# Retention and two feed-forward layers on one core: weight steps freed from program order, the first weight loads moved, the tail of v in tiles of its own

## The chip, the cores and the metric

One core of a Trainium2 chip. The metric is the device time of one execution in microseconds; the median of several executions counts. The profile is of one execution, and its span runs from the first to the last instruction.

## The reference

A retention block feeds two feed-forward layers. For batch 4, 8 heads, 576 positions and head size 64, `scores = q k^T / 8` is multiplied by a lower-triangular table of powers of a decay (one for each head), and the product is multiplied by `v`. The heads are laid side by side, which makes `x` of 2304 tokens by 512. Then:

```python
h = x @ w_in                                   # 512 x 2048
g = (a0 + a1*h + a2*h**2 + a3*h**3) / (1 + abs(b0)*abs(h) + abs(b1)*h**2 + 1e-6)
x = g @ w_out                                  # 2048 x 512
h = x @ w2_in
g = s * maximum(h, 0)**2 + b
out = g @ w2_out
```

q, k, v and the result are float32; the four weight matrices come as float64 and are cut by the kernel into two parts (wh and wl) whose sum carries the precision, as the activations are.

## The kernel before, in words

**Retention.** Work goes by pairs of heads: 16 pairs (4 batches by 4 pairs), and two neighbouring pairs form a group that is loaded together, 8 groups in all. `loads(g)` (L320) takes the tiles of group g from pools of three buffers and issues 15 DMAs on SyncE's queue: for k, q and v four loads of 128 positions by 4 heads (L196), and one load for the last 64 positions, the tail (L203). The tails of k and q lie in one tile (`raw_t`, 64 rows each). The tail of v is loaded as the last 128 positions (S - 128 to S) into a fifth chunk of v's tile; its first 64 rows are positions that the fourth chunk holds already, and the mask makes them count for nothing. `scale(p)` (L212) multiplies the v of a pair by its decay on GpSimd, all five chunks in one instruction. The loop over pairs (L357) then does, for pair p, in this order: load group p/2 + 2 (for even p), the state's part of the values (`value_state`, L294), the transpositions of pair p + 2 (tails first, L229, then k and q, L224) with its scaling, the sums of pair p + 1 (`state`, L268, with copies on ScalarE, L282, and sums on VectorE, L284), the values (`value_chunk`, L306, and the scaled outputs on VectorE, L308 and L309), the scores of pair p + 1 (L247, L249) and their masks on VectorE (L253, L256). PE's and VectorE's instructions of this part are pinned.

**Pins.** The kernel is written in a framework that puts the instructions of each engine in order at build, by a simulated timeline: an instruction that is ready there may be put before others that stand ahead of it in the program. `keep_in_program_order` pins an instruction behind the one that was written just before it on its engine. A pinned instruction cannot come before that one; if that one is not pinned itself, both may be put forward together.

**Weights.** One weight tile is 128 columns of w_in with the 128 rows of w_out that belong to them, 1 MB of float64; there are 16 for each layer, 32 in all. `w_load(kf)` (L96) issues two DMAs of 512 KB on SyncE (L100, L102) into one of two raw buffers. `w_cut(kf)` (L104) turns the raw tile into wh and wl in five steps, a generator that stops after each: ScalarE's Abs (L116) and VectorE's clamp of the low words (L117); VectorE's L119 and L120; L122; L125; then ScalarE's copy to wh (L132), GpSimd's difference wl (L133), and the load of the next tile, which takes the raw buffer that is now free. One buffer `wm` holds the intermediate value.

The first three tiles are cut within the retention, one call of the generator at the end of each pair from pair 2 on, all steps pinned. The last stop of one tile runs on into the first step of the next, so a tile takes four calls and three tiles take 13. The loads of the first two tiles stand in pair 0 behind `loads(2)`, the third group (L360). Four small loads (`small_loads`, L314) of parameters stand in pair 2; from them come `babs` (L599, ScalarE) and `aneg` (L600, VectorE), which are written after the retention and not pinned. Tiles 3 to 31 are cut within the feed-forward, where `emit_cuts` (L549) spreads the steps over the units of work; there L116, L117 and L119 are pinned, the others are not.

**Feed-forward.** A unit is one block of 512 (or 256) tokens with one weight tile: 12 matmuls in (L412 to L414), the function on ScalarE, VectorE and GpSimd (L429 to L463, or L465 to L473), 12 matmuls out (L497). In the function of the first layer, L453 is VectorE's last read of the PSUM tile that a later unit's L412 needs.

Of the kernel before, what the change touches and what calls it, by code (L numbers as in the profile page):

```python
# [10 lines left out]
F32 = mybir.dt.float32  # L11
# [5 lines left out]
ALU = mybir.AluOpType  # L17
# [13 lines left out]
RAW_BUFS = 2  # L31
# [4 lines left out]
W_FIRST = 3  # L36
# [4 lines left out]
def retention_ffn_kernel(ctx, tc, q, k, v, w_in1, w_out1, a, b, w_in2, w_out2, s2, b2, maskv, gdec, out):  # L41
    nc = tc.nc
    B, H, S, D = q.shape
    NT, DM = out.shape
    DFF = w_in1.shape[1]
    P = 128
# [3 lines left out]
    NCH = (S + P - 1) // P  # L50
    TAIL = S - (NCH - 1) * P
    NMAIN = S // P
# [23 lines left out]
    def f32(t):  # L76
        return t.bitcast(F32)
# [8 lines left out]
    def next_load():  # L86
        if w_ahead:
            w_load(w_ahead.pop(0))
# [15 lines left out]
    def w_cut(kf, pinned=False):  # L104

        words = w_raw.pop(kf).rearrange("p w n -> p (w n)").bitcast(I32).rearrange("p (n two) -> p n two", two=2)
        lo, hi = words[:, :, 0].bitcast(U32), words[:, :, 1]
        f = hi.bitcast(F32)  # L110
        m = wtmp.tile([P, 2 * DM], F32, tag="wm", name=f"wm{kf}")
        t = m.bitcast(I32)

        pin = tc.keep_in_program_order
        rest = pin if pinned else lambda ins: ins
        pin(nc.scalar.activation(m, f, AF.Abs))  # L116
        pin(nc.vector.tensor_scalar(lo, lo, 2.0 ** 28, 2.0 ** 32 - 256, op0=ALU.add, op1=ALU.min))  # L117
        yield
        pin(nc.vector.tensor_scalar(m, m, 2.0 ** -15, None, op0=ALU.max))  # L119
        rest(nc.vector.tensor_scalar(t, t, 5, 2, op0=ALU.logical_shift_left, op1=ALU.logical_shift_right))  # L120
        yield
        rest(nc.vector.scalar_tensor_tensor(out=t, in0=hi, scalar=-0x40000000, in1=t,  # L122
                                            op0=ALU.bitwise_and, op1=ALU.bitwise_or))
        yield
        rest(nc.vector.scalar_tensor_tensor(out=hi.bitcast(U32), in0=lo, scalar=29, in1=t.bitcast(U32),  # L125
                                            op0=ALU.logical_shift_right, op1=ALU.bitwise_or))
        yield
        wh, wl = w_slots[kf % W_BUFS]
        whf, wlf = (x.rearrange("p w c f -> p (w c f)") for x in (wh, wl))
        for which in range(2):  # L130
            w_t[kf, which] = (wh[:, which], wl[:, which])
        nc.scalar.copy(whf, f)  # L132
        nc.gpsimd.tensor_tensor(out=wlf, in0=f, in1=f32(whf), op=ALU.subtract)  # L133
        next_load()
# [8 lines left out]
    def retention(actx):  # L143

        sb1 = actx.enter_context(tc.tile_pool(name="sb1", bufs=1))
# [7 lines left out]
        NM = NMAIN * P  # L153
        mv = sb1.tile([P, P + TAIL + NCH * H + NP], F32, name="mv")
        mask, tmask = mv[:, 0:P], mv[:, P:P + TAIL]
        vdec = mv[:, P + TAIL:P + TAIL + NCH * H].rearrange("p (c h) -> p c h", c=NCH)
# [8 lines left out]

        assert 2 * TAIL == P and NCH == NMAIN + 1 and NP % 2 == 0
        tiles, xT, pm, pv = {}, {}, {}, {}

        def raw(nm, p):

            h = 2 * (p % 2)
            return tiles[nm, p // 2][:, :, h:h + 2, :]

        def flat(t):
            return t.rearrange("p h d -> p (h d)")


        def pe(ins):
            tc.keep_in_program_order(ins)
# [1 line left out]
        dve = pe  # L181

        def load_tiles(g):
            for nm, n in (("k", NMAIN), ("q", NMAIN), ("v", NCH), ("t", 1)):
                tiles[nm, g] = sbr.tile([P, n, 4, D], F32, tag=f"raw_{nm}", name=f"raw_{nm}{g}")

        def load(nm, g, part, eng=nc.sync):

            bb, h0 = pairs[2 * g][0], 2 * pairs[2 * g][1]
            src = {"q": q, "k": k, "v": v}[nm]  # L190
            t = tiles[nm, g]
            hs = range(4) if part is None else range(2 * part, 2 * part + 2)
            h1, h2 = hs[0], hs[-1] + 1
            if part is None:
                for c in range(NMAIN):
                    eng.dma_start(out=t[:, c], in_=src[bb, h0:h0 + 4, c * P:(c + 1) * P, :].rearrange("h p d -> p h d"))  # L196
            else:
                for j in hs:
                    eng.dma_start(out=t[:, 0:NMAIN, j, :],
                                      in_=src[bb, h0 + j, 0:NM, :].rearrange("(c p) d -> p c d", p=P))  # L200
            s0 = S - P if nm == "v" else NM
            o = t[:, NMAIN] if nm == "v" else tiles["t", g][0:TAIL, 0] if nm == "k" else tiles["t", g][TAIL:P, 0]
            eng.dma_start(out=o[:, h1:h2, :], in_=src[bb, h0 + h1:h0 + h2, s0:S, :].rearrange("h p d -> p h d"))  # L203

        def decay_table():

# [4 lines left out]

        def scale(p):  # L212
            hp = pairs[p][1]
            t = raw("v", p)
            nc.gpsimd.tensor_tensor(out=t, in0=t, op=ALU.mult,
                                    in1=vdec[:, :, 2 * hp:2 * hp + 2].unsqueeze(3).to_broadcast([P, NCH, 2, D]))

        def transpose(p):
            o = xT[p]
# [76 lines left out]

        def value_chunk(p):
            bb, hp = pairs[p]
            vn = raw("v", p)
            for c in range(NCH):  # L300
                n = min(P, S - c * P)
                for j in range(2):
                    r = slice(64 * j, 64 * j + 64)
                    o = pv[p][r, c * P:c * P + n] if c < NMAIN else out_tail[r]
                    rh = pm[p, j][:, c * P:c * P + n] if c < NMAIN else pm[p, 2][:, j, :]
                    pe(nc.tensor.matmul(o, lhsT=vn[:, c, j, :], rhs=rh, start=False, stop=True, skip_group_check=True))  # L306
            x = sbt.tile([P, S], F32, tag="x", bufs=2, name=f"x{p}")
            dve(nc.vector.tensor_tensor(out=x[:, NM:S], in0=out_tail, in1=odec[:, hp, NM:S], op=ALU.mult))  # L308
            dve(nc.vector.tensor_tensor(out=x[:, 0:NM], in0=pv[p], in1=odec[:, hp, 0:NM], op=ALU.mult))  # L309
            xs = slice(bb * S, (bb + 1) * S)  # L310
            nc.scalar.copy(xh[:, hp, xs], x)
            nc.gpsimd.tensor_tensor(out=xl[:, hp, xs], in0=x, in1=f32(xh[:, hp, xs]), op=ALU.subtract)
# [44 lines left out]
        for p in range(NPAIR):  # L357
            if p % 2 == 0:
                loads(p // 2 + 2)
            if p == 0:  # L360
                for _ in range(RAW_BUFS):
                    next_load()
            if p == 2:
                small_loads()
            value_state(p, range(1, NMAIN))
            if 0 < p < NPAIR - 2:
                transposes(p + 2)
            value_state(p, [NMAIN])
            if p + 1 < NPAIR:
                state(p + 1)  # L370
            value_chunk(p)
            if p + 1 < NPAIR:
                scores(p + 1)
            if p == 0:
                transposes(2)
            if p > 1:
                next(steps, None)
        for _ in steps:
            pass
# [217 lines left out]
    with ExitStack() as actx:  # L597
        retention(actx)
# [49 lines left out]
```

## Time and profile before

| | us |
|---|---|
| median of 3 runs | 941.04 (940.54 to 942.96) |
| the profiled execution | 942.34 |
| its span | 940.1 |
| PE busy in the span | 896.5 (95%) |
| VectorE, ScalarE, GpSimd busy | 619.3, 556.4, 357.7 |
| mean granted clock of PE | 0.983 |

In the profile PE is the matmuls, PEld the weight loads into PE, DVE is VectorE, ACT is ScalarE, POOL is GpSimd and SP is SyncE, whose whole work here is to issue DMAs (SPq). L12 is line 12. A row of the timeline gives the start, the duration, the engine, the line and the operation with the names of what it writes and reads; in brackets stands how long the engine was idle before it and what ended that. Rows of the same kind that follow each other are merged (x4). [...]

### The profile page before, as it was taken

To read this page: it belongs to the slowest core of one execution; us is meant where nothing else is said; L and a number is where in the kernel's file an instruction comes from. 1 tells how busy PE (TensorE), PEld (TensorE's weight loads), DVE (VectorE), ACT (ScalarE), POOL (GpSimd) and SP (SyncE) were. 2 spreads that over 40 slices of the span, in tenths; PEclk is the share of its full clock that TensorE was granted. 3 is DMA by queue.
4 is the path that set the end of the run, shared out by engine and by line. 5 is a ranking of instruction groups with operands and counts; after the bars stand their busy time and mean duration, and the time that the engine had idled before them with its cause. 6 is when DMAs were issued, how large, how long until landed. Compare 5 with 4: busy or idle time off the path is not lost.

```text
span 940.1 us, 12896 instructions
## 1 busy us (share of the span) xinstructions
PE 896.5 (95%) x4912; PEld 756.0 (80%) x4912; DVE 619.3 (66%) x965; ACT 556.4 (59%) x940; POOL 357.7 (38%) x256
## 2 busy tenths in 40 slices
PE   7799899999999989999799999999999999999998
PEld 6688778888787868888588878888888888888886
DVE  2476679688796796988688984446555555554344
ACT  3354389796777677777768864544444443443332
POOL 4355457456474454665557871111111111110000
PEclk9899899999999989999999999999999999999999
DMA  8978112011110111100111111111111102100013
GB/s 190 230 165 199 43 46 83 7 46 45 36 35 20 46 45 46 45 26 21 46 45 45 46 45 46 45 45 46 45 45 45 45 2 89 45 0 1 1 68 134
DMA packets 84716, 54.16 MB, mean 58 GB/s; under 512 B 61232, under 2 KB 78256, under 8 KB 84656
## 3 DMA queue, kind: packets, MB, share of 16 engines
q1 hardware_dynamic: 82784, 52.68, 19.0%
q10 hardware_dynamic: 1872, 0.68, 0.3%
q8 instruction: 38, 0.62, 0.3%
q14 instruction: 22, 0.18, 0.1%
HBM read 48.62 MB, written 4.72 MB: 57 GB/s over the span
## 4 chain that ended last, share of the span: by engine, by line
PE 74%; DVE 9%; ACT 5%; POOL 4%; issue 3%; SPq 2%; DMA 2%; DVEq 0%; POOLq 0%; ACTq 0%
PE o L497 34%; PE h L412 12%; PE h L413 12%; PE h L414 12%; POOL tq L434 2%; DVE acc L509 2%; SPq L196 2%; PE pv L306 1%; DVE tt L451 1%; PE b_sum L268 1%; DVE h L452 1%; PE sc L247 1%; PE pv L294 1%; DVE wm L122 1%; POOL wl L133 1%
## 5 line engine op out<-in xcount | busy, mean ns | idle before, releaser
L412 PE MATMUL h<-xl,wh 128*128 128x512 f32 (+1 forms) x640 | 236.8, 372 | 9.8 <-DVE tt L453 9.7
L413 PE MATMUL h<-xh,wl 128*128 128x512 f32 (+1 forms) x640 | 237.2, 371 | 1.4 <-POOL wl L133 1.4
L414 PE MATMUL h<-xh,wh 128*128 128x512 f32 (+1 forms) x640 | 237.0, 370 | 0.0
L133 POOL TENSOR_TENSOR wl<-raw,wh 128x1024 fp32r<-128x1024 f32 x32 | 78.3, 2446 | 292.5 <-ACT wh L132 151.7
L412 PEld LDWEIGHTS h<-xl,wh 128*128 128x128 f32 x640 | 121.4, 190 | 32.5 <-DVE tt L453 4.0
L434 POOL TENSOR_TENSOR tq<-tq,ta 128x512 f32<-128x512 f32 (+1 forms) x80 | 100.8, 1262 | 111.4 <-ACT tq L433 104.4
L413 PEld LDWEIGHTS h<-xh,wl 128*128 128x128 f32 x640 | 121.5, 190 | 23.6 <-POOL wl L133 2.8
L468 ACT ACTIVATE ta<-h 128x512 f32<-128x512 f32 (+1 forms) x80 | 44.2, 555 | 161.0 <-PE h L414 160.3
L414 PEld LDWEIGHTS h<-xh,wh 128*128 128x128 f32 x640 | 121.5, 190 | 20.6
L470 DVE TENSOR_SCALAR tt<-ta,s_sb,b_sb 128x512 f32<-128x512 f32 (+1 forms) x80 | 45.1, 566 | 137.6 <-ACT ta L469 137.4
L497 PE MATMUL o<-gl,wh 128*128 128x512 f32 (+1 forms) x320 | 119.5, 374 | 6.5 <-POOL gl L463 5.0
L463 POOL TENSOR_TENSOR gl<-tt,gh 128x512 fp32r<-128x512 f32 (+1 forms) x80 | 105.5, 1321 | 46.1 <-ACT gh L458 37.3
L497 PE MATMUL o<-gh,wl 128*128 128x512 f32 (+1 forms) x320 | 118.4, 370 | 0.0
L497 PE MATMUL o<-gh,wh 128*128 128x512 f32 (+1 forms) x320 | 117.9, 369 | 0.0
L497 PE MATMUL o<-wh,gl 128*128 128x512 f32 x288 | 112.1, 389 | 0.0
L497 PE MATMUL o<-wh,gh 128*128 128x512 f32 x288 | 112.1, 389 | 0.0
L473 DVE TENSOR_TENSOR gl<-tt,gh 128x512 fp32r<-128x512 f32 (+1 forms) x80 | 69.5, 870 | 42.6 <-ACT gh L472 42.6
L497 PE MATMUL o<-wl,gh 128*128 128x512 f32 x288 | 93.1, 390 | 1.4 <-DVE acc L509 1.4
L509 DVE TENSOR_TENSOR acc<-acc,o 128x512 f32<-128x512 f32 (+1 forms) x114 | 70.1, 650 | 12.0 <-PE o L497 12.0
L440 DVE TENSOR_TENSOR tt<-tt,h 128x512 f32<-128x512 f32 (+1 forms) x80 | 50.1, 627 | 41.4 <-ACT tt L435 41.3
L497 PEld LDWEIGHTS o<-gl,wh 128*128 128x128 f32 x320 | 60.6, 189 | 19.5 <-POOL gl L463 6.6
L451 DVE SCALAR_TENSOR_TENSOR tt<-tt,aneg,h 128x512 f32<-128x512 f32 (+1 forms) x80 | 55.0, 687 | 28.4 <-ACT h L446 28.4
(74 smaller groups left out, 1514.1 us busy)
## 6 DMA issues: line engine op xcount, KB each, us to landing
raw<-in_moe_w_in_dram SPq DMA_DIRECT2D x32, 512.0 KB, 3.9
raw<-in_moe_w_out_dram SPq DMA_DIRECT2D x32, 512.0 KB, 4.8
raw_v<-in_v_dram SPq DMA_DIRECT2D x39, 128.0 KB, 3.0
out_dram<-acc SPq DMA_DIRECT2D x18, 256.0 KB, 2.1
raw_k<-in_k_dram SPq DMA_DIRECT2D x32, 128.0 KB, 3.2
raw_q<-in_q_dram SPq DMA_DIRECT2D x30, 128.0 KB, 3.0
raw_t<-in_k_dram SPq DMA_DIRECT2D x7, 64.0 KB, 3.3
raw_t<-in_q_dram SPq DMA_DIRECT2D x7, 64.0 KB, 3.4
```

What stands on the lines that cost most here:

```text
L133: nc.gpsimd.tensor_tensor(out=wlf, in0=f, in1=f32(whf), op=ALU.subtract)
L412: nc.tensor.matmul(ps, lhsT=wh[:, c, :], rhs=xl[:, c, r], start=c == 0, stop=False)
L413: nc.tensor.matmul(ps, lhsT=wl[:, c, :], rhs=xh[:, c, r], start=False, stop=False)
L414: nc.tensor.matmul(ps, lhsT=wh[:, c, :], rhs=xh[:, c, r], start=False, stop=c == NC - 1)
L434: nc.gpsimd.tensor_tensor(out=tq, in0=tq, in1=ta, op=ALU.mult)
L440: nc.vector.tensor_tensor(out=tt, in0=tt, in1=h, op=ALU.mult)
L451: nc.vector.scalar_tensor_tensor(out=tt, in0=tt, scalar=aneg[:, 0:1], in1=r, op0=ALU.add, op1=ALU.mult)
L463: nc.gpsimd.tensor_tensor(out=gl, in0=tt, in1=f32(gh), op=ALU.subtract)
L470: nc.vector.tensor_scalar(tt, ta, s2_sb, b2_sb, op0=ALU.mult, op1=ALU.add)
L473: nc.vector.tensor_tensor(out=gl, in0=tt, in1=f32(gh), op=ALU.subtract)
L497: nc.tensor.matmul(ps, lhsT=lh, rhs=rh, start=st and x == 0, stop=sp and x == 2)
L509: nc.vector.tensor_tensor(out=at, in0=at, in1=ps, op=ALU.add)
```

## The change

Three edits. (1) In `w_cut` the pins of L116, L117 and L119 hold only for tiles 0 to 4 (`W_FIRST + RAW_BUFS` is 5); the steps of tiles 5 to 31 are not pinned at all. (2) In the retention's loop the first two weight loads go from pair 0 to pairs 3 and 5, the small loads from pair 2 to pair 7, and the steps of the first three tiles begin at pair 5 (one call a pair up to pair 11, two from pair 12 on: 15 calls). (3) The tail of v is loaded as its 64 positions alone, into rows 64 to 127 of three standing tiles that are cleared once at the start; the scaling becomes two instructions, one for four chunks and one for the tail.

```diff
@@ w_cut
-        pin = tc.keep_in_program_order
-        rest = pin if pinned else lambda ins: ins
+        def free(ins):
+            return ins
+
+        rest = tc.keep_in_program_order if pinned else free
+        pin = tc.keep_in_program_order if kf < W_FIRST + RAW_BUFS else free
@@ retention
+        vtail = [sb1.tile([P, 4, D], F32, name=f"vtail{i}") for i in range(3)]
+        for t in vtail:
+            nc.gpsimd.memset(t[0:P - TAIL], 0.0)
+        def tail_of(p):
+            h = 2 * (p % 2)
+            return vtail[p // 2 % 3][:, h:h + 2, :]
@@ load_tiles
-            for nm, n in (("k", NMAIN), ("q", NMAIN), ("v", NCH), ("t", 1)):
+            for nm, n in (("k", NMAIN), ("q", NMAIN), ("v", NMAIN), ("t", 1)):
@@ load
-            s0 = S - P if nm == "v" else NM
-            o = t[:, NMAIN] if nm == "v" else tiles["t", g][0:TAIL, 0] if nm == "k" else tiles["t", g][TAIL:P, 0]
-            eng.dma_start(out=o[:, h1:h2, :], in_=src[bb, h0 + h1:h0 + h2, s0:S, :].rearrange("h p d -> p h d"))
+            o = vtail[g % 3][P - TAIL:] if nm == "v" else tiles["t", g][0:TAIL, 0] if nm == "k" else tiles["t", g][TAIL:P, 0]
+            eng.dma_start(out=o[:, h1:h2, :], in_=src[bb, h0 + h1:h0 + h2, NM:S, :].rearrange("h p d -> p h d"))
@@ scale
-            t = raw("v", p)
+            t, vt = raw("v", p), tail_of(p)[P - TAIL:]
             nc.gpsimd.tensor_tensor(out=t, in0=t, op=ALU.mult,
-                                    in1=vdec[:, :, 2 * hp:2 * hp + 2].unsqueeze(3).to_broadcast([P, NCH, 2, D]))
+                                    in1=vdec[:, 0:NMAIN, 2 * hp:2 * hp + 2].unsqueeze(3).to_broadcast([P, NMAIN, 2, D]))
+            nc.gpsimd.tensor_tensor(out=vt, in0=vt, op=ALU.mult, in1=vdec[P - TAIL:, NMAIN, 2 * hp:2 * hp + 2]
+                                    .unsqueeze(2).to_broadcast([TAIL, 2, D]))
@@ value_chunk
-            vn = raw("v", p)
+            vn, vt = raw("v", p), tail_of(p)
-                    pe(nc.tensor.matmul(o, lhsT=vn[:, c, j, :], rhs=rh, start=False, stop=True, skip_group_check=True))
+                    pe(nc.tensor.matmul(o, lhsT=vn[:, c, j, :] if c < NMAIN else vt[:, j, :], rhs=rh,
+                                        start=False, stop=True, skip_group_check=True))
@@ the loop over pairs
-            if p == 0:
-                for _ in range(RAW_BUFS):
-                    next_load()
-            if p == 2:
+            if p in (3, 5):
+                next_load()
+            if p == 7:
                 small_loads()
@@
-            if p > 1:
+            for _ in range((p > 4) + (p > 11)):
                 next(steps, None)
```

## Rows read from the trace of the kernel before

**Rows 1.** Stretches: us; PE, PEld, DVE, ACT, POOL busy (instructions); PEclk; DMA share; GB/s:
```profile
0.00:116.82 116.82, 96.78 (x1168) 88.72 (x1168) 65.52 (x145) 49.64 (x104) 54.06 (x46) 0.93 0.72 166
116.82:560.00 443.18, 424.10 (x2013) 353.43 (x2012) 364.18 (x551) 344.01 (x571) 271.88 (x198) 0.98 0.12 41
```

**Rows 2.** Timeline of PE in the retention: L229 opens a pair's transpositions:
```profile
33.88 0.27 PE L229 MATMUL trt<-ident,raw_t 128*128 128x128 f32 x1
...
44.18 0.45 PE L229 MATMUL trt<-ident,raw_t 128*128 128x128 f32 x1 [2.88 <-DMA raw_t<-in_q_dram]
...
51.62 0.27 PE L229 MATMUL trt<-ident,raw_t 128*128 128x128 f32 x1
...
56.85 0.29 PE L229 MATMUL trt<-ident,raw_t 128*128 128x128 f32 x1
...
79.39 0.27 PE L229 MATMUL trt<-ident,raw_t 128*128 128x128 f32 x1
...
93.27 0.27 PE L229 MATMUL trt<-ident,raw_t 128*128 128x128 f32 x1
...
98.83 0.69 PE L294 MATMUL b_out<-xT,spad 128*128 128x64 f32 x2 [4.28 <-DVE pmt L253]
...
105.14 0.27 PE L229 MATMUL trt<-ident,raw_t 128*128 128x128 f32 x1
```

**Rows 3.** Timeline of SyncE's queue, 0 to 112 us:
```profile
20.24 2.16 SPq L196 DMA_DIRECT2D raw_k<-in_k_dram  x4
...
28.89 0.52 SPq L100 DMA_DIRECT2D raw<-in_moe_w_in_dram  x1
...
31.29 5.66 SPq L196 DMA_DIRECT2D raw_k<-in_k_dram  x4
...
44.85 0.50 SPq L315 DMA_DIRECT2D a_sb<-in_moe_a_dram  x1
...
92.52 0.37 SPq L100 DMA_DIRECT2D raw<-in_moe_w_in_dram  x1
```

**Rows 4.** Busy time by stretch, 31.2 to 36 us (columns as in rows 1):
```profile
31.20:36.00 4.80, 4.80 (x69) 4.39 (x67) 2.95 (x8) 1.28 (x4) 3.87 (x3) 1.00 0.98 348
```

**Rows 5.** Timelines of ScalarE, VectorE and GpSimd in the retention:
```profile
36.45 1.20 ACT L116 ACTIVATE wm<-raw 128x1024 f32<-128x1024 f32 x1 [1.94 <-DMA raw<-in_moe_w_out_dram]
...
47.74 0.76 DVE L600 TENSOR_SCALAR aneg<-a_sb 128x4 f32<-128x4 f32 x1 [3.75 <-DMA a_sb<-in_moe_a_dram]
...
97.95 0.70 DVE L117 TENSOR_SCALAR raw<-raw 128x1024 uint32<-128x1024 uint32 x1 [5.50 <-DMA raw<-in_moe_w_out_dram]
...
87.19 2.94 POOL L215 TENSOR_TENSOR raw_v<-raw_v,mv 128x640 f32<-128x640 f32 x2 [6.41 <-PE trt L229]
```

**Rows 6.** Line L203, the tails' loads: issue ns min/median/max; time to landing:
```profile
L203 SPq DMA_DIRECT2D raw_t<-in_k_dram x9: 607/607/2019, 1.8 to 74.5; - x9
L203 SPq DMA_DIRECT2D raw_v<-in_v_dram x9: 368/505/1612, 4.9 to 88.9; - x9
...
DMA to landing us min/median/max: 2.3/3.2/6.8
```

**Rows 7.** First layer: waits in total, VectorE's and PE's timeline, sum at half clock:
```profile
PE h L412 <- DVE tt L453: 9.7, 5, 3.7
...
323.11 0.68 DVE L119 TENSOR_SCALAR wm<-wm 128x1024 f32<-128x1024 f32 x1
...
325.57 1.66 DVE L122 SCALAR_TENSOR_TENSOR wm<-raw,wm 128x1024 int32<-128x1024 int32 x1
...
333.21 0.77 PE L412 MATMUL h<-xl,wh 128*128 128x512 f32 x1 [3.65 <-DVE tt L453]
...
sum 13.65, PE 12.55 PEld 9.19 DVE 13.65 ACT 8.38 POOL 10.36; mean PE 4.18 PEld 3.06 DVE 4.55 ACT 2.79 POOL 3.45
```

**Rows 8.** Timeline of GpSimd at the start of the retention:
```profile
8.21 1.04 POOL L209 TENSOR_TENSOR odec<-odec,mv 128x512 f32<-128x512 f32 x1 [6.02 <-DMA raw_v<-in_v_dram]
9.21 1.26 POOL L215 TENSOR_TENSOR raw_v<-raw_v,mv 128x640 f32<-128x640 f32 x1
```

## The prediction, made before the change was run

> **What bounds the kernel now.** I read the busy time by stretch first [rows 1]. The program has three stretches: the retention (0 to 116.82 us), the first feed-forward layer (to about 560 us) and the second. In the third PE is busy throughout, so nothing in this change can move it. In the first layer PE is busy 424.10 of 443.18 us: 19.1 us idle. In the retention PE is busy 96.78 of 116.82 us and the granted clock is 0.93 in the mean.
>
> Then I followed one mark of the retention, the transposition of the tails (L229), which opens the PE work of each pair of heads [rows 2]. From 51.62 to 56.85 a pair takes 5.23 us with no wait; I take that as the unhindered pair. Against it three places lose time. A: from 33.88 to 51.62 two pairs take 17.74 us, 7.28 too many, with a wait of 2.88 us for the tail of q and a granted clock of one half behind it. B: from 51.62 to 79.39 five pairs take 27.77 us (1.62 too many) and from 79.39 to 93.27 two take 13.88 (3.42 too many), 5.04 together; it falls at the two changes of weight tile. C: from 93.27 to 105.14 one pair takes 11.87 us, 6.64 too many, with a wait of 4.28 us for VectorE's L253.
>
> The queue of SyncE says why A happens [rows 3]. Loads are issued there one behind the other without a pause from the start to about 89 us. The first two weight tiles are issued at 28.89, between the third group of heads and the fourth; the four loads of k that follow take 5.66 us to issue where the group before took 2.16, since the transfers are full (348 GB/s, share 0.98 [rows 4]). ScalarE too waits 1.94 us there for the first weight tile before its first step on it [rows 5].
>
> C is seen on VectorE and GpSimd [rows 5]. At 97.95 VectorE has waited 5.50 us for the weights of the fourth tile (L117), and the masks of the scores (L253, pinned) stand behind it. Its code stands after the retention, but it is pinned only behind L600, which depends on one small load and ran at 47.74; so the build's scheduler was free to put it forward. Its load was issued at 92.52 [rows 3], when GpSimd had finished L133 of the second tile; GpSimd had itself waited 6.41 us until 87.19 at the scaling of v in front of it.
>
> **The change, part by part.**
>
> *Weight loads behind the groups.* The four weight loads leave the place before the fourth group; the tile 0 pair comes behind that group, the tile 1 pair behind the fifth. A should go: 7.28 us. What comes in its place is a smaller lateness later. The fourth group is then issued from 28.9 to about 37.5 (as the third: 20.24 to 28.89, 8.65 us), tile 0 to 38.6, and the last load that pair 8's transpositions need is through 5.5 us on (2.16 for each four of k and q, 0.61 for each tail [rows 3, 6]), at 44.1. With 3.2 us to landing (the median of the tails [rows 6]) and 1.05 MB of weights ahead of it at 348 GB/s (3.0 us), it lands at 50.3. Without a wait PE wants it two pairs after pair 6's mark, which would stand at 33.88 + 5.23 = 39.1, so at 49.6. That is 0.7 us late; between 0 (the transfers overlap better) and 7.28 (all of A comes back one group later) I take 1.0.
>
> *Small loads moved from pair 2 to pair 7.* Four issues of at most 0.50 us [rows 3] leave the place before the fifth group and stand before a later one: no gain in sum. But L600 waits for one of them on VectorE: 3.75 us at 47.74 [rows 5], which cost nothing there, because PE was behind with A. That cover goes with A. Behind L600 on VectorE stand the state's sums and the masks, on which PE waits. Bounds 0 and 3.75; I take 1.5, since L600 may also be placed well after the landing.
>
> *One step a pair from pair 5, two from pair 12.* The 15 calls do the same work as the 14 before. The change of tile (copy of wh, then Abs of the next tile, both on ScalarE) still comes twice within the retention, so B stays: 0. VectorE is busy 65.52 us in the retention [rows 1], 4.1 for each of 16 pairs, a step's work included; a second step of up to 1.66 (L122 [rows 7]) makes 5.8 where a pair has 5.23. Three pairs have two steps with work for VectorE: between 0 and three whole steps (5.0 us); by the overrun 1.6, of which I take 1.0, since other pairs give some back.
>
> *Fourth tile's load.* It now follows the second tile's end at pair 12 instead of pair 10, when the loads of v are through earlier and GpSimd should not hold L133 back. L117 of this tile keeps its pin behind L600 alone, so it can still be put forward into the retention, and the load needs about 5 us (issued 92.52, the wait ended 97.95). C can stay whole (6.64) or go (0). I take 2.0 left: 4.64 gained.
>
> *Tail of v as 64 rows.* By bytes this halves nine loads of together 1.05 MB: 0.5 MB, 3.2 us at the stretch's 166 GB/s. By rows it saves nothing: the tails of k, which already are 64 rows, take 607 ns to issue in the median where the tail of v with 128 rows takes 505 [rows 6], so nine loads are 0.9 us dearer at SyncE. I take 0, between -3.2 and +0.9. [...] On GpSimd the scaling of 640 columns (1.26 us) becomes one of 512 (1.04 for a product of that size) [rows 8] and a small one; by proportion of columns 0.26, at most 0.5. GpSimd is busy 54.06 of 116.82 us, its idle hides that. The three clearings at the start lie before the first load lands. The tail matmuls keep their shape.
>
> *Pins off from the sixth tile.* In the first layer four kinds of PE waits make up the 19.1 us; the largest is five waits of together 9.7 us for L453 on VectorE [rows 7]. The longest of these, 3.65 us before 333.21, comes behind a bunch: L119 of a weight tile at 323.11, released from its pin, and L120, L122 and L125 at once after it, over 4 us of weight work within 6 us. With the pin gone these can be placed when the tile has landed, in VectorE's gaps. The clock stood at one half for 13.65 us, with PE busy 12.55 of it: at full clock 6.3 us less [rows 7]. So 9.7 + 6.3 = 16.0 us hang on such bunches, with 25.4 (19.1 + 6.3) as the most that could go; the other end is a loss (below). A new order will make bunches of its own, so I take 6.5, some two fifths.
>
> **Sum.** Retention: 7.28 - 1.0 - 1.5 - 1.0 + 4.64 = 8.4 us. First layer: 6.5 us. Together 14.9 us off the profiled execution's 942.34 (its span is 940.1, the 2.2 around it stay), 927.4; that execution lies 1.3 us above the median of the runs, 941.04, so the median should be 926.
>
> **The rivals.**
>
> *The loads don't move (935 us).* Weight loads depend on nothing but a free buffer. If the scheduler finds SyncE idle before the fourth group's buffers are free, it puts them in front as before, and A stays. For it: the fourth tile's L117 was put forward in just this way [rows 5]. Against: the small loads, free as well, did not pass the fourth group [rows 3]. Only the first layer's 6.5 us would remain: 941 - 6.5 = 934.5.
>
> *The first layer gains nothing (933 us).* The weight work is the same amount on an engine that is busy 364.18 of 443.18 us; bunches may fall elsewhere. For it: the waits come where blocks of 256 columns follow each other, which stay. Then 941.0 - 8.4 = 932.6.
>
> *An unpinned step waits for its load on VectorE (955 us, slower).* The trace has one example of what an early L117 does: C, 5.50 us of wait and 6.64 us of PE's time [rows 2, 5]. Eleven tiles of the first layer lose their pins. If the scheduler takes each load as landed some microseconds too soon, each blocks VectorE. VectorE has 79.0 us free in 443.18, 4.9 for each of 16 tiles; the case decides once the wait uses that up. At a third of C's price: 11 x 6.64 / 3 = 24 us, against 8.4 gained in the retention, and 941 + 24 - 8 = 957, or 955 where some are absorbed. Against it: C's wait came from transfers that were full, and in the first layer their share is 0.12 [rows 1].
>
> **How the numbers follow.** The forecast (both gains in part, 926) has 0.50, the first rival 0.15, the second 0.20, the third 0.12; 0.03 is left for both gains failing, about 940. A measurement of this kernel can tell 0.3% (2.8 us) from no change. The forecast and the first two rivals are faster by more than that, but at their poor ends touch the bound: I move 0.04 from there to the same side. Faster 0.81, same 0.07, slower 0.12. The range: its lower end is A and C wholly gone with no new lateness (13.9) and the 16.0 of the bunches, 911; its upper end 941, where the first two rivals are inside and the third is left out.
>
> **What would show it.** Right: on SyncE the fourth group directly behind the third with no slow issues; no wait of PE for the tail of q near 40 us; two pairs there in about 10.5 us; the feed-forward's first matmul near 108 to 109 us; PE idle in the first layer near 14 us, and fewer microseconds at half clock. Wrong: weight loads again at 29 us; L117 waiting in front of L253; L600 with a wait and PE idle behind it; tail loads of v issued in half the time (then the transfers did get shorter); in the first layer VectorE's L117 or ScalarE's L116 waiting for the raw weights tile after tile.

## The result, and the profile after

The changed kernel takes 926.63 us (median of 4 runs, 926.3 to 927.15) against 941.48 for the kernel before in the same session (940.54 to 942.96): a ratio of 0.9841 [0.9824, 0.9858]. Its profiled execution takes 926.35, with a span of 924.2 us. Predicted were 926. The number is right and the way to it is not: the retention gave 2.65 us where 8.4 were expected, the feed-forward 13.2 where 6.5 were.

The lines of the changed file stand lower: L116, L117, L119, L120, L122, L125 are now L119, L120, L122, L123, L125, L128; the tails' load L203 is L212, the tail transposition L229 is L240, L412 is L423, L453 is L464, and `babs` and `aneg` are L610 and L611.

Busy time of the changed kernel by stretch, columns as in [rows 1]; its feed-forward begins at 114.17 (before: 116.82), its first layer ends at 544:

```profile
0.00:114.17 114.17, 95.96 (x1169) 88.33 (x1169) 64.43 (x145) 47.66 (x102) 56.27 (x64) 0.93 0.72 166
114.17:544.00 429.83, 418.44 (x2015) 350.89 (x2014) 371.75 (x561) 346.38 (x573) 282.99 (x199) 1.00 0.13 45
544.00:924.20 380.20, 375.31 (x1733) 313.29 (x1731) 170.22 (x261) 161.44 (x266) 28.28 (x13) 1.00 0.12 41
```

The first layer takes 429.83 us instead of 443.18 [rows 1]. PE's idle time in it is 11.39 (429.83 - 418.44) instead of 19.08, which is 7.7 us. The other 5.7 are busy time (424.10 - 418.44): the granted clock stands at 0.50 for 3.41 us behind 129.02, where it did so for 13.65 in all before [rows 7]. With PE busy for 3.41 and 12.55 us of that, half of the difference, 4.6 us, is the clock's by my estimate: in the changed kernel a 128x512 matmul starts every 0.43 us at 0.50 (129.41 to 131.97) and every 0.23 at 1.00 (132.65 to 133.80). The retention is as long as before within 2.65 us, with the same mean clock of 0.93.

PE's timeline of the changed kernel, the marks of the pairs (L240) and the waits among them:

```profile
20.53 0.45 PE L240 MATMUL trt<-ident,raw_t 128*128 128x128 f32 x1 [3.01 <-DMA raw_t<-in_q_dram]
...
35.47 0.27 PE L240 MATMUL trt<-ident,raw_t 128*128 128x128 f32 x1
...
45.98 0.27 PE L240 MATMUL trt<-ident,raw_t 128*128 128x128 f32 x1
...
53.38 0.30 PE L240 MATMUL trt<-ident,raw_t 128*128 128x128 f32 x1 [2.02 <-issue]
60.16 0.27 PE L240 MATMUL trt<-ident,raw_t 128*128 128x128 f32 x1
66.27 0.30 PE L240 MATMUL trt<-ident,raw_t 128*128 128x128 f32 x1 [0.72 <-DMA raw_t<-in_q_dram]
69.17 0.66 PE L235 MATMUL trq<-ident,raw_q 128*128 128x128 f32 x4 [2.15 <-ACT xT L241]
73.77 0.27 PE L240 MATMUL trt<-ident,raw_t 128*128 128x128 f32 x1
...
87.63 0.27 PE L240 MATMUL trt<-ident,raw_t 128*128 128x128 f32 x1
...
98.08 0.27 PE L240 MATMUL trt<-ident,raw_t 128*128 128x128 f32 x1
104.30 0.32 PE L260 MATMUL b_out<-xT 64*128 64x64 f32 x1 [1.86 <-DVE x L320]
114.17 0.50 PE L423 MATMUL h<-xl,wh 128*128 128x512 f32 x1
127.51 0.50 PE L423 MATMUL h<-xl,wh 128*128 128x512 f32 x1 [2.15 <-DVE tt L464]
```

Against the unhindered pair of 5.23 us, each stretch between marks is two pairs (10.46). A is gone: 35.47 to 45.98 is 10.51. 45.98 to 60.16 is 14.18, 3.72 too many; 60.16 to 73.77 is 13.61, 3.15 too many; 73.77 to 87.63 is 13.86, 3.40 too many; C is gone: 87.63 to 98.08 is 10.45. From 98.08 to the feed-forward are 16.09 us, where the same piece took 11.68 before (105.14 to 116.82 [rows 2]).

SyncE's queue in the changed kernel, for [rows 3]:

```profile
29.60 2.19 SPq L206 DMA_DIRECT2D raw_k<-in_k_dram  x4
...
39.43 0.60 SPq L100 DMA_DIRECT2D raw<-in_moe_w_in_dram  x1
40.08 0.50 SPq L102 DMA_DIRECT2D raw<-in_moe_w_out_dram  x1
40.68 4.35 SPq L206 DMA_DIRECT2D raw_k<-in_k_dram  x4
45.07 2.02 SPq L212 DMA_DIRECT2D raw_t<-in_k_dram  x1
47.14 3.28 SPq L206 DMA_DIRECT2D raw_q<-in_q_dram  x4
50.47 0.61 SPq L212 DMA_DIRECT2D raw_t<-in_q_dram  x1
...
63.99 0.60 SPq L327 DMA_DIRECT2D a_sb<-in_moe_a_dram  x1
```

The fourth group (29.60) follows the third without a weight load and with quick issues of k; its four loads of q take 3.24 us (from 32.48) where the third group's take 2.25. The slowest issues now stand behind the first weight tile one group later: the fifth group's four loads of k take 4.35 us, its tail of k 2.02 instead of 0.61.

Two steps of the changed kernel that wait for the small loads, ScalarE's and VectorE's:

```profile
68.06 0.20 ACT L610 ACTIVATE babs<-b_sb 128x2 f32<-128x2 f32 x1 [5.00 <-DMA b_sb<-in_moe_b_dram]
66.83 0.17 DVE L611 TENSOR_SCALAR aneg<-a_sb 128x4 f32<-128x4 f32 x1 [2.29 <-DMA a_sb<-in_moe_a_dram]
```

The totals of waits in the changed kernel's first layer (us in total, times, longest):

```profile
DVE raw L120 <- DMA raw<-in_moe_w_out_dram: 17.5, 12, 3.8
ACT wm L119 <- DMA raw<-in_moe_w_out_dram: 8.1, 7, 1.6
PE h L423 <- DVE tt L464: 5.2, 3, 2.6
```

The third rival's sign is there: the freed steps L119 and L120 wait for their raw tile in many of the tiles (VectorE twelve times). Yet PE's waits for L464 fell from 9.7 [rows 7] to 5.2. This is what the experiments had to take apart.

### The profile page after: what moved, and what is told of

Read it like the earlier page. It is cut to its first block, busy times and chain, and to the rows that moved or that the text cites. A ratio compares the mean times of both kernels' runs of the same rounds, so it can differ in the third digit from the quotient of the medians.

```text
span 924.2 us, 12932 instructions
## 1 busy us (share of the span) xinstructions
PE 889.7 (96%) x4912; PEld 752.5 (81%) x4912; DVE 606.4 (66%) x965; ACT 555.5 (60%) x940; POOL 367.5 (40%) x275
## 4 chain that ended last, share of the span: by engine, by line
PE 55%; DVE 15%; POOL 5%; ACT 4%; DMA 4%; issue 3%; SPq 0%; DVEq 0%; POOLq 0%; ACTq 0%
PE o L508 28%; PE h L425 9%; PE h L423 9%; PE h L424 9%; DMA raw<-in_moe_w_out_dram 4%; POOL wl L136 2%; DVE wm L125 2%; DVE raw L128 2%; DVE acc L520 2%; DVE tt L462 1%; DVE wm L122 1%; DVE h L463 1%; POOL tq L445 1%; DVE tt L451 1%; DVE tt L452 1%
## 5 line engine op out<-in xcount | busy, mean ns | idle before, releaser
L423 PE MATMUL h<-xl,wh 128*128 128x512 f32 (+1 forms) x640 | 236.6, 370 | 5.5 <-DVE tt L464 5.2
L445 POOL TENSOR_TENSOR tq<-tq,ta 128x512 f32<-128x512 f32 (+1 forms) x80 | 105.9, 1324 | 106.5 <-ACT tq L444 99.7
L481 DVE TENSOR_SCALAR tt<-ta,s_sb,b_sb 128x512 f32<-128x512 f32 (+1 forms) x80 | 47.2, 589 | 148.2 <-ACT ta L480 147.8
L423 PEld LDWEIGHTS h<-xl,wh 128*128 128x128 f32 x640 | 120.7, 189 | 27.9 <-DVE tt L464 7.3
L484 DVE TENSOR_TENSOR gl<-tt,gh 128x512 fp32r<-128x512 f32 (+1 forms) x80 | 53.1, 664 | 40.3 <-ACT gh L483 40.3
L483 ACT CAST gh<-tt 128x512 fp32r<-128x512 f32 (+1 forms) x80 | 46.3, 579 | 55.0 <-DVE tt L481 53.0
L456 ACT ACTIVATE ta<-tq,lnb 128x512 f32<-128x512 f32 (+1 forms) x80 | 54.5, 683 | 26.0 <-POOL tq L445 25.7
```

Of the source, the lines that this page charges most:

```text
L423: nc.tensor.matmul(ps, lhsT=wh[:, c, :], rhs=xl[:, c, r], start=c == 0, stop=False)
L445: nc.gpsimd.tensor_tensor(out=tq, in0=tq, in1=ta, op=ALU.mult)
L456: nc.scalar.activation(ta, tq, AF.Ln, bias=lnb, scale=QS)
L481: nc.vector.tensor_scalar(tt, ta, s2_sb, b2_sb, op0=ALU.mult, op1=ALU.add)
L483: nc.scalar.copy(gh, tt)
L484: nc.vector.tensor_tensor(out=gl, in0=tt, in1=f32(gh), op=ALU.subtract)
```

## The experiments

All twelve in one table: median, ratio to the kernel before on the same chip with its interval, the profile's start of the feed-forward (its first matmul), the time from there to the end of the span, and PE's idle time in the first 429.8 us of it (429.8 less PE's busy time there). The kernel before took 941.5, 942.3, 942.4 and 941.4 us (medians) in the four sessions, so differences between sessions are good to about 1 us.

| run | us | ratio | start | rest | PE idle |
|---|---|---|---|---|---|
| before | 941.48 | 1 | 116.82 | 823.3 | 17.7 |
| after | 926.63 | 0.984 [0.982, 0.986] | 114.17 | 810.0 | 11.4 |
| e1 pins alone | 929.47 | 0.987 [0.985, 0.989] | 116.60 | 814.2 | 12.4 |
| e2 loads alone | 938.60 | 0.996 [0.994, 0.997] | 114.26 | 822.8 | 18.9 |
| e3 tail of v alone | 938.95 | 0.996 [0.995, 0.998] | 119.01 | 816.8 | 15.6 |
| e4 loads and tail | 938.76 | 0.995 [0.994, 0.997] | 115.89 | 824.2 | 18.1 |
| e5 after, babs and aneg pinned | 929.62 | 0.986 [0.985, 0.987] | 111.60 | 817.1 | 15.7 |
| e6 after, first step pinned | 916.50 | 0.972 [0.971, 0.973] | 114.18 | 800.9 | 4.4 |
| e7 after without the tail's edit | 923.34 | 0.980 [0.978, 0.981] | 112.64 | 808.6 | 10.4 |
| e8 after, last step split | 921.82 | 0.978 [0.977, 0.980] | 107.89 | 811.8 | 12.2 |
| e9 e6 and e8 without the tail's edit | 915.42 | 0.973 [0.971, 0.974] | 108.92 | 803.9 | 6.8 |
| e10 e9 and e5 | 914.20 | 0.971 [0.969, 0.973] | 110.26 | 801.7 | 5.6 |
| e11 before, third pin off alone | 915.61 | 0.972 [0.971, 0.974] | 114.98 | 797.5 | 2.8 |
| e12 e6 and e8 | 914.46 | 0.971 [0.970, 0.973] | 106.21 | 804.3 | 6.6 |

### The three edits by themselves

**e1**, the first edit of the diff in the kernel before, nothing else:

```diff
-        pin = tc.keep_in_program_order
-        rest = pin if pinned else lambda ins: ins
...
+        rest = tc.keep_in_program_order if pinned else free
+        pin = tc.keep_in_program_order if kf < W_FIRST + RAW_BUFS else free
```

> The kernel before with the first edit alone (pins of the weight steps off from the sixth tile). Theory (each edit has its own place): all of the first layer's gain, 13 us by the spans from the feed-forward's first matmul on, is this edit's, and the retention stays as before (first matmul at about 117 us): 928 us. Rival (the build puts the whole program in a new order, so the gain belongs to the three edits together): the first layer's idle time of PE stays near 19 us, 938 to 943 us. Rival of the prediction's third kind (steps that wait for their loads cost time): over 941 us.

929.47 us (928.8 to 932.6), 12.9 less than before in that session (942.33). The retention is unchanged (116.60); the rest is 9.1 us shorter in the profiled execution, which with 932.6 is the longest of these. So most of the whole change's gain is in this edit, as the theory had it.

**e2**, the second edit alone:

```diff
-            if p == 0:
-                for _ in range(RAW_BUFS):
-                    next_load()
-            if p == 2:
+            if p in (3, 5):
+                next_load()
+            if p == 7:
...
-            if p > 1:
+            for _ in range((p > 4) + (p > 11)):
```

> The kernel before with the second edit alone (weight loads behind the fourth and fifth group, small loads at pair 7, steps from pair 5). Theory: the feed-forward's first matmul comes some 3 to 5 us earlier (112 to 114 us), the first layer keeps 19 us of PE idle: 937 to 938 us. If the later start of the second group's work in the changed kernel (PE wait of 3 us at 20 us) comes from this edit, it shows here; if from the tail of v, PE's wait at 20 us is 0.9 as before.

938.60, 3.7 less, a little above the expected time. The feed-forward starts 2.56 us earlier and is no shorter.

**e3**, the third edit alone:

```diff
...
-            s0 = S - P if nm == "v" else NM
...
+            o = vtail[g % 3][P - TAIL:] if nm == "v" else ...
...
```

> The kernel before with the third edit alone (tail of v as 64 rows in standing tiles). Theory (half the rows take as long): no change by time, 940 to 942 us, SyncE's tails of v dearer by 0.1 us each. Rival (half the bytes): loads end up to 3 us earlier and the retention is 1 to 3 us shorter, 938 to 940 us. If PE's wait at 20 us grows to 3 us, this edit is its cause.

938.95, 3.4 less, though its retention is 2.2 us longer; neither expectation fits. The gain is in the feed-forward (816.8 against 823.3), in which this edit changes nothing: what is left is another order of the build, which I take as the cause and no run shows. With this edit PE waits over 2 us at the start of the third pair; the kernel before waits 0.86 there, e7 hardly. PE's timeline of e3, and of e7 (below), which has the two other edits:

```profile
20.21 0.30 PE L237 MATMUL trt<-ident,raw_t 128*128 128x128 f32 x1 [2.08 <-DMA raw_t<-in_q_dram]
```

```profile
20.16 0.33 PE L232 MATMUL trt<-ident,raw_t 128*128 128x128 f32 x1
```

**e4**, the second and the third edit, the pins as before:

```diff
...
-        pin = tc.keep_in_program_order if kf < W_FIRST + RAW_BUFS else free
+        pin = tc.keep_in_program_order
...
```

> The changed kernel with the first edit undone (all tiles pinned as before). Theory (additive): the retention as in the changed kernel (first matmul of the feed-forward at 114 us), the first layer with 19 us of PE idle again: 938 to 940 us. Rival (gain belongs to the edits together): 930 us or less.

938.76, 3.6 less, as the theory had it, with the start at 115.89 instead of 114; the pair's wait near 20 us is there again (2.79). The parts don't add: 12.9, 3.7 and 3.4 make 20.0 where the whole gives 14.9, and e2's and e3's 7.1 come to 3.6 together.

### The terms of the retention

**e5**, the changed kernel with the two steps on the small loads pinned:

```diff
-    nc.scalar.activation(babs, b_sb, AF.Abs)
-    nc.vector.tensor_scalar(aneg, a_sb, -1.0, None, op0=ALU.mult)
+    tc.keep_in_program_order(nc.scalar.activation(babs, b_sb, AF.Abs))
+    tc.keep_in_program_order(nc.vector.tensor_scalar(aneg, a_sb, -1.0, None, op0=ALU.mult))
```

> The changed kernel with babs and aneg pinned where they are written, behind the retention. Theory (the small loads' uncovered wait costs 3.15 us between pair 9's and pair 11's marks, on ScalarE 5.0 us and on VectorE 2.3): the waits of PE at 66 and 69 us go, these two pairs take 10.5 us instead of 13.6, the first matmul of the feed-forward comes near 111 us, 923 to 924 us. Rival (PE waits there for the loads of the sixth group, so the same time is lost to them): pair 11's mark stays at 73 to 74 us, 926 to 927 us.

PE's timeline of e5:

```profile
60.84 0.27 PE L240 MATMUL trt<-ident,raw_t 128*128 128x128 f32 x1
...
71.92 0.27 PE L240 MATMUL trt<-ident,raw_t 128*128 128x128 f32 x1
...
125.55 0.50 PE L423 MATMUL h<-xl,wh 128*128 128x512 f32 x1 [2.77 <-DVE tt L464]
```

The two pairs take 11.08 instead of 13.61: the small loads' term is 2.5 us, shown, and the start of the feed-forward comes 2.57 earlier. But the kernel is slower and not faster, 929.62: 3.0 us by the medians, 2.1 by the differences to the kernel before, and the intervals of the ratios overlap. The feed-forward is 7.1 us longer (817.1 against 810.0), and why is not shown. So the expected 923 to 924 is missed, though what was expected of the retention came.

**e7**, the changed kernel without its third edit (the tail of v as before):

```diff
...
-            o = vtail[g % 3][P - TAIL:] if nm == "v" else ...
+            s0 = S - P if nm == "v" else NM
...
```

> The changed kernel with the third edit undone (tail of v as 128 rows, one scaling). Theory (the tail edit costs 1 to 2 us in the retention by dearer issues and by the second scaling instruction, and gains nothing): PE's wait at 20 us is 0.7 to 0.9 us, the first matmul of the feed-forward at 112.5 to 114.5 us, 924 to 927 us. Rival (half the bytes help later): 928 us or more.

923.34, 3.3 us less than the changed kernel; the feed-forward starts 1.53 earlier. In the changed kernel the tail's edit is a loss. It is not one everywhere: in the kernel before it gained 3.4 (e3), and with e6 and e8 the kernel that has it is 1.0 faster than the one without (e12 and e9 below), which is within the noise.

**e8**, the changed kernel with one more stop at the end of the five steps, so that a tile's last step and the next tile's first do not come in one call:

```diff
         next_load()
+        yield
```

> The changed kernel with one more stop in a weight tile's steps, so that the copy to wh of one tile and the Abs of the next no longer come in one call (15 calls do all, as the changed loop has them). Theory (the change of tile costs 3.4 us in pairs 11 to 13 and some 2.5 at the end, because ScalarE does both in a row before its copies of the state): the waits of 1.7 and 1.9 us for VectorE's L320 go, the first matmul of the feed-forward comes at 110 to 112 us, 922 to 924 us. Rival (VectorE is the one that is late): same waits, 926 to 927 us.

The start comes 6.28 us earlier (107.89), more than was expected, the total falls by 4.8 (921.82); PE waits 4.52 us at 123.58. The mark of the last pair in PE's timeline of e8:

```profile
95.96 0.27 PE L241 MATMUL trt<-ident,raw_t 128*128 128x128 f32 x1
```

From there to the feed-forward are 11.93 us, where the changed kernel takes 16.09: 4.16 of the 6.28. In the changed kernel ScalarE's copy of the state (L293) stands at 102.84 behind the copy to wh and the next tile's Abs, and PE waits 1.86 us at 104.30; in e8 it stands at 98.32, in front of both, and PE waits 0.15. Another 1.5 us of the lead is there at pair 4's mark (28.70 against 30.19), before any weight step: that part is not the split's.

### Which pin it is

**e6**, the changed kernel with the pins of the first step (L119, L120) on for all tiles, so that from the sixth tile on only the maximum (L122) is free of those that were pinned:

```diff
-        pin = tc.keep_in_program_order if kf < W_FIRST + RAW_BUFS else free
+        pin = tc.keep_in_program_order
+        mid = tc.keep_in_program_order if kf < W_FIRST + RAW_BUFS else free
...
-        pin(nc.vector.tensor_scalar(m, m, 2.0 ** -15, None, op0=ALU.max))
+        mid(nc.vector.tensor_scalar(m, m, 2.0 ** -15, None, op0=ALU.max))
```

> The changed kernel with the first step (ScalarE's Abs, VectorE's clamp) pinned again in all tiles, and only the next operation (the maximum, before L119) left free from the sixth tile on. Theory (the gain came from the third pin, which held the whole rest of a tile's work back until its deadline): the first layer as in the changed kernel, PE idle near 12 us, 925 to 929 us, with no waits for loads on VectorE. If the loads' waits (28.8 us on VectorE, 23.8 on ScalarE) cost something, this is faster than the changed kernel by 1 to 4 us. Rival (the early first step is what matters): PE idle near 19 us again, 936 to 940 us.

916.50: 10.1 us faster than the changed kernel, where at most 4 were expected, with the same start (114.18). The waits for raw tiles are gone from its first layer.

**e11**, the same two lines in the kernel before, without the second and the third edit:

> The kernel before with nothing but the third pin (the maximum, before L119) taken off from the sixth tile on. Theory (this pin alone held the tiles' work back to their deadlines, and the first two pins keep steps from waiting for loads): retention as before (first matmul at 116 to 118 us), PE idle in the feed-forward 4 to 8 us, no wait for weight loads behind 120 us: 918 to 924 us, faster than the first edit alone (929.5). Rival (the first step must be free too for the gain): 930 us or more.

915.61, 25.8 us under the kernel before (941.41 in that session) and 11.0 under the changed one, from one freed instruction a tile; that is below the expected 918 to 924. Busy time by stretch in e11, and PE's waits in the first layer, all of 1 us or more in total:

```profile
0.00:114.98 114.98, 92.71 (x1168) 84.67 (x1168) 63.23 (x145) 49.42 (x104) 54.00 (x46) 0.96 0.73 169
114.98:558.20 443.22, 440.39 (x2127) 370.95 (x2126) 378.71 (x569) 354.15 (x592) 270.99 (x199) 1.00 0.13 43
```

```profile
PE h L417 <- POOL wl L137: 1.5, 1, 1.5
PE o L501 <- POOL gl L467: 1.2, 1, 1.2
```

In 443.22 us, as long as the whole first layer was before, PE is idle for 2.8, and the clock stays at 1.00. A and C are both still in its retention (waits of 3.56 us at 43.86 and 4.62 at 97.63). What the freed maximum does is seen at one tile, on VectorE's timeline of e11 and of the kernel before:

```profile
287.15 0.69 DVE L121 TENSOR_SCALAR raw<-raw 128x1024 uint32<-128x1024 uint32 x1
289.08 0.91 DVE L123 TENSOR_SCALAR wm<-wm 128x1024 f32<-128x1024 f32 x1
...
292.70 1.99 DVE L129 SCALAR_TENSOR_TENSOR raw<-raw,wm 128x1024 uint32<-128x1024 uint32 x1
```

```profile
289.89 0.68 DVE L117 TENSOR_SCALAR raw<-raw 128x1024 uint32<-128x1024 uint32 x1
300.37 0.68 DVE L119 TENSOR_SCALAR wm<-wm 128x1024 f32<-128x1024 f32 x1
...
307.27 1.21 DVE L125 SCALAR_TENSOR_TENSOR raw<-raw,wm 128x1024 uint32<-128x1024 uint32 x1
```

The clamp (L121, L117) comes at about the same time in both. In e11 the maximum follows 1.9 us behind it and the tile is done at 294.7; before, the pinned maximum (L119) came 10.5 us behind it and the tile was done at 308.5. Over fourteen tiles from the sixth on, the maximum starts 7.0 us behind the clamp in the mean in the kernel before and 2.9 us in e11, by VectorE's timelines. From the maximum to the end of the tile it is 7.2 us before and 7.5 in e11: the steps stand as close together as they did, only earlier.

The waits of VectorE and ScalarE for raw tiles in the whole feed-forward of e1, where all three pins are off:

```profile
DVE raw L120 <- DMA raw<-in_moe_w_out_dram: 32.8, 22, 4.1
ACT wm L119 <- DMA raw<-in_moe_w_out_dram: 24.5, 19, 3.5
```

In e11 VectorE's and ScalarE's steps have none behind 120 us. So freeing the first step costs 13.9 us (e1 less e11) in the one surrounding and 10.1 (after less e6) in the other. The runs don't separate what of this is the waits themselves and what the order that the build makes around them; a kernel with the first step free and its tile always loaded (another raw buffer) wasn't tried.

One order of the build could be luck, but the fourteen kernels of the table fall into three groups by their pins alone, whatever the other edits are. With all three pinned (before, e2, e3, e4) they take 938.6 us or more; with all three free (after, e1, e5, e7, e8) 921.8 to 929.6; with the maximum alone free (e6, e9 to e12) 914.2 to 916.5. PE's idle time follows: 15.6 us or more, 10.4 to 15.7, and 2.8 to 6.8.

### Does an earlier start pay through?

**e9** is e6 and e8 together without the third edit, **e10** is e9 with e5's pins, **e12** is e6 and e8 with the third edit; their lines are those shown above.

> First step pinned in all tiles, the extra stop between two tiles, v's tail as before. Theory (the three findings are in different places and add up): the retention as with the extra stop or a little earlier (first matmul at 107 to 110 us), PE idle in the feed-forward 4 to 8 us: 908 to 913 us. Rival (each build's order decides, parts don't add): 915 us or more.

> The same with babs and aneg pinned behind the retention. Theory (the small loads' wait holds PE up by 2 to 3 us in the retention; what the run with these pins alone lost came from the feed-forward's new order and from first steps waiting for loads, which are pinned here): 2 to 3 us faster than the kernel without these pins. Rival (PE only waits elsewhere, or the feed-forward's order turns out worse again): the same or slower by up to 4 us.

> The changed kernel with the first step pinned in all tiles and the extra stop; v's tail as 64 rows. Theory (the tail edit costs 1 to 3 us in the retention's start): 1 to 3 us slower than the same without the tail edit, PE's wait near 20 us at 2 to 3 us against 0.9 or less. Rival (tail edit neutral, differences between builds are the order's): within 1 us of it or faster.

They take 915.42, 914.20 and 914.46. In each the rival held rather than the theory: the findings don't add up (e9), the small loads' pins give 1.2 us, which is within the noise (e10), and the tail's edit loses nothing (e12). Their starts lie 4.7 to 8.8 us ahead of e11's, their totals at most 1.4 under it; the intervals of the ratios overlap. All four beat both kernels; e11 does it with the smallest edit. In e12, at the start of the feed-forward, ScalarE's timeline, PE's, and the stretch behind:

```profile
111.38 1.13 ACT L136 CAST wh<-raw 128x1024 fp32r<-128x1024 f32 x1 [0.46 <-DVE raw L129]
112.41 1.14 ACT L120 ACTIVATE wm<-raw 128x1024 f32<-128x1024 f32 x1
113.57 0.60 ACT L445 ACTIVATE ta<-h 128x512 f32<-128x512 f32 x1
```

```profile
121.75 0.79 PE L425 MATMUL h<-xl,wh 128*128 128x512 f32 x1 [4.36 <-DVE tt L466]
```

```profile
120.93:127.75 6.82, 6.00 (x14) 4.74 (x15) 6.79 (x11) 5.89 (x11) 3.80 (x3) 0.50 0.01 2
```

ScalarE's timeline of e11 at the same step:

```profile
118.23 0.60 ACT L436 ACTIVATE ta<-h 128x512 f32<-128x512 f32 x1 [1.54 <-POOL xl L316]
```

e12's first matmul is 8.77 us ahead of e11's, its first step of the function only 4.66 (113.57 against 118.23): the third tile's copy and the fourth tile's Abs stand in front of it on ScalarE. Then PE waits 4.36 us for VectorE's L466, and about the wait's end the clock is at 0.50 for 6.82 us, which by the same estimate costs half of the 6.00 that PE is busy there, 3.0. Wait and half clock, 7.4 us, are most of the lead; e11 has no half clock there and waits 1.16 us at 130.44. The runs between agree: in the ten with the second edit the wait for the same step is 4.36 to 4.56 us long behind the starts of 106.2 to 108.9, 3.31 behind 110.26, 2.77 behind 111.60 and 1.64 to 2.17 behind 112.6 to 115.9; the four without that edit don't have it there, so that it goes with that edit as well as with the earlier start. I read this as a lead that ScalarE and VectorE can't take up; that it goes is shown, its cause is only argued from these rows.

## Why the number was right and the steps were not

**A: right.** 7.28 us gone, and the fourth group stands directly behind the third on SyncE, with its issues of k quick and those of q not.

**The lateness behind it: 1.0 taken, 3.7 measured.** Here the step "is through 5.5 us on, at 44.1" failed. It took quick issues (2.16 for four loads) behind the weight tile; they were slow as A's had been, and the load was through at 51.08 (50.47 + 0.61). PE's mark stood at 53.38 behind 2.02 us of idle. The row names no releaser; that it is this load is read from its landing, 2.8 us behind the start of its issue, at 53.27. The bounds 0 and 7.28 held; the row that it is nearest to was A's own slow issue [rows 3], and I took the quick one.

**Small loads: 1.5 taken, 3.15 in that stretch, 2.5 of it shown by e5.** The step named VectorE's `aneg` alone. ScalarE's `babs`, also unpinned, waited 5.00 us for its load with the copies of the transpositions (L241) behind it, and PE 2.15 us for those.

**Double steps and the change of tile: 1.0 and 0 taken.** B was to stay (5.04); its second half is now 3.40 and its first half lies in the stretches above. But the last change of tile and the pairs with two steps lie at the end, which is 4.4 us longer. e8, which only splits the change of tile, makes this end 4.16 us shorter: the change of tile, taken at 0, is nearly all of it.

**C: 4.64 gained by the prediction, 6.64 measured.** No wait is left at that place (10.45 us for two pairs). The step "it can still be put forward into the retention" was right, and yet it cost nothing. The fourth tile's load is issued at 104.40, later than before (92.52) and not earlier, and VectorE's clamp stands one pair further on, where its tile has landed, so that no wait is shown in front of it; the masks follow at 111.45:

```profile
110.84 0.69 DVE L120 TENSOR_SCALAR raw<-raw 128x1024 uint32<-128x1024 uint32 x1
```

**Tail of v: no saving, as taken, but a later start that the sum lacks.** The changed kernel's loads of the tails, issue in ns min/median/max, for [rows 6]:

```profile
L212 SPq DMA_DIRECT2D raw_t<-in_k_dram x9: 607/607/2025, 1.8 to 75.1; - x9
L212 SPq DMA_DIRECT2D vtail<-in_v_dram x9: 607/607/612, 4.9 to 87.8; - x9
```

The 64 rows took 607 ns to issue in the median, as the tails of k did, dearer than the 128 rows before (505). And the new tails, half the bytes, land no sooner. The 3.2 of [rows 6] is the median of all tails, of k and q too; by tile the medians from issue to landing, in us, are, of the changed kernel and of the kernel before, where the row holds v's other loads too:

```profile
vtail<-in_v_dram SPq DMA_DIRECT2D x7, 64.0 KB, 3.0
```

```profile
raw_v<-in_v_dram SPq DMA_DIRECT2D x39, 128.0 KB, 3.0
```

At 3.0 us for either size these rows show no saving by half the bytes, but they don't show the transfer by itself: that it saves 0, as the sum took it, was an estimate that no run shows. The dearer issue says nothing of the transfer.

What the sum didn't have is that pair 4's mark comes 1.62 us later, behind a wait of 3.01 for the tail of q at 20.53, which was 0.86 before. The wait is this edit's: all seven kernels that have it wait there (1.32 to 3.01), the seven others 0.91 at most. In the changed kernel PE is there 1.6 us sooner (17.52, by start less wait, against 19.14), and the load is issued 0.54 later (16.32 against 15.78); two tails of v ahead of it on SyncE take 0.61 us each to issue where they took 0.37 and 0.51. The later mark is not the wait's alone: e5, e6 and e8 have the wait and pair 4's mark at 28.68 to 28.77, where it was 28.57 before. In the changed kernel the granted clock is 0.50 from 20 to 26 us, in e5 and e8 1.00; why it falls in one and not in the other is open.

The measured terms close: 7.28 - 3.72 - 3.15 + 1.64 (B) + 6.64 - 4.41 - 1.62 = 2.66, against 2.65 by the two starts.

**Pins: 6.5 taken, 13.2 measured.** That the pins hold the steps back to a bad time was right, and of the three it is the maximum's: e11 frees it alone, and the waits for L453 and the half clock of the first layer are gone. The bunch itself [rows 7] is not the cause that the prediction took it for: in e11 the steps stand as close together (7.5 us from the maximum to the end, 7.2 before), but 4.1 us sooner behind the clamp. Why they hold up L453 less there is not shown. The size was off, since "some two fifths" of 16.0 was a guess between ends. With the maximum alone, 25.8 us go from the feed-forward (823.3 to 797.5), about the 25.4 that the prediction gave as the most.

**The slower rival was half right.** Its mechanism acts: 17.5 us of waits on VectorE in twelve places of the first layer. Its price, 24 us, was too high (10 to 14 by e6 and e11). What stood against it, that C's wait came from full transfers, is not shown: before the change the DMA share was 0.55 from 92.50 to 97.95, C's wait; and in the changed kernel's first layer VectorE waited at a mean share of 0.13. The rival's cost is there, but it came together with a gain that is larger. It was written as an alternative to the gain; it is a term beside it.

So 926 came out because a gain too large in the retention (8.4 for 2.65) and one too small in the first layer (6.5 for 13.2) nearly balance; that they do is luck.

## What to carry to other kernels

When a change frees several instructions of a chain from program order, price each by itself: here the one in the middle gave 25.8 us, and freeing the first, which waits for a load, gave 10 to 14 of them back. A stall that is taken away from a prologue is worth only what the next stage can take up; look at which engine that stage's first step waits for before the gain is counted. And where a build orders instructions anew, time a part of a change also together with the rest: 20.0 us of single gains were 14.9 in sum, and an edit of the retention moved the feed-forward by 6.5.

## What the runs showed of the chip

A tail of v with half the bytes was no cheaper at SyncE's queue but dearer, 607 ns against 505. Behind 512 KB weight loads the next group's issues were slow in both kernels: four loads of k took 5.66 us behind two pairs before and 4.35 behind one pair after, where the four loads of k one group earlier took 2.16 and 2.19. Issues were slow without them too (3.24 us for the changed kernel's four loads of q at 32.48). And a wait of PE can cost more than itself: about the end of e12's wait of 4.36 us the granted clock was 0.50 for 6.82 us, behind the changed kernel's 2.15 us at 127.51 for 3.41. Not every wait does: behind the changed kernel's 2.57 us at 178.18 and e5's 2.77 at 125.55 the clock stayed at 1.00. e11's first layer, without a wait over 1.54 us, has no half clock.
